# Who adds the two halves of a head pair's output: one addition of each pair moved from GpSimd to VectorE

## The chip, the cores and the metric

The kernel runs on one core of a Trainium2 chip. The time is the device time of one execution in microseconds (us). Each kernel is timed several times, and the median counts. Beside that, one execution is recorded by the hardware profiler. The engines are TensorE (PE; PEld is its loading of weights), VectorE (DVE), ScalarE (ACT), GpSimd (POOL) and SyncE (SP), which issues the DMAs.

## What is computed

Two layers, each an attention block and a gated MLP block with a mixing over the sequence, over 2048 tokens of width 640. The change touches attention only. It has 32 heads of 20 numbers, and the 2048 tokens are cut into 4 segments of 512. Within a segment attention is causal softmax; across segments a memory M is read.

```python
for s in range(N):                       # 4 segments
    qs, ks, vs = q[:, :, s], k[:, :, s], v[:, :, s]
    logits = jnp.einsum("bhqd,bhkd->bhqk", qs, ks) * scale + mask
    p = _softmax(logits, axis=-1)
    a_dot = jnp.einsum("bhqk,bhkd->bhqd", p, vs)
    pq = phi(qs)
    num = jnp.einsum("bhld,bhde->bhle", pq, M)
    den = jnp.einsum("bhld,bhd->bhl", pq, z)[..., None] + 1e-6
    a_mem = num / den
    o = g * a_mem + (1.0 - g) * a_dot
    outs.append(o)
    pk = phi(ks)
    M = M + jnp.einsum("bhld,bhle->bhde", pk, vs)
    z = z + jnp.einsum("bhld->bhd", pk)
```

## The kernel before

Each layer runs three stages one after the other: attention (phase1a), the MLP's input half (phase1b) and its spatial half with the output (phase2). Some work of phase1b is already placed into the end of attention.

Attention goes over 64 pairs of heads per layer: segment by segment, and in a segment through 16 pairs. Two pairs take five steps (the loop over t in `run`). For each pair TensorE makes the scores twice. Once by queries (`by_queries`), into the PSUM tile mp, of which there is one buffer; VectorE takes the row maxima of it (mxs, lines 956 and 959). These are turned on TensorE (mtp), split into two float16 parts (mr, ScalarE and VectorE) and written by DMA into spare rows of qk, so that the second making of the scores, by keys (`by_keys`, into es), has the maximum already subtracted. ScalarE takes the exponential of es into P (line 933). P is float32; it is split into two float16 parts, PH by ScalarE (line 968) and the rest PL = P - PH by GpSimd (line 970, two instructions of 128x640 for each head, so four for a pair; the last two pairs of a layer's second heads are done by VectorE). TensorE multiplies PH and PL with the values (`pvs`, line 998) into the PSUM tile pv, one buffer, 41 columns for each head and block of 128 queries: 20 columns of the values' high part, one column of sums of P, and 20 columns of the values' low part.

`combine` makes a pair's output from pv. VectorE scales the sums (rs, line 1009), inverts them (1010) and multiplies all of pv by them into ab in SBUF (1014). With a the first 20 columns of ab and b the last 20, the output is a + b, plus what was read from the memory if the segment isn't the first. The memory's part lies already in the group's tile gm (`read`, written by VectorE at line 834), of which o is the pair's slice. GpSimd does both additions: line 1017 adds o to a (only for segments after the first), line 1018 puts a + b into o. When the last pair of a group of 6 or 8 heads is done, `out` splits gm into two float16 parts, ohl (ScalarE at line 1026, GpSimd at line 1027), and SP stores them (line 1030).

Between these steps TensorE gets filler: the projections of queries and keys (kps, qps), of values (vps) and of the output (yps), the memory's update (mup) and reading (num). VectorE and ScalarE finish each of them (qhl, khl, relu, phq, phl, vs). Layernorm of coming rows is spread over VectorE, ScalarE and GpSimd as well (lnst, lnrs, xnhl).

TensorE's order in attention is that of the program. The order on the other engines comes from the scheduler, which works with its own model of time: where an instruction is moved or gone, others may change places. Each engine then works through its own order and waits at each instruction for what it needs.

Of the kernel before, what the change touches and what calls it, by code (L numbers as in the profile page):

```python
# [14 lines left out]
ALU = mybir.AluOpType  # L15
# [578 lines left out]
class Attention:  # L594
# [407 lines left out]
    def combine(self, n, s, m, h0):  # L1002
        g, nc = self.g, self.nc
        T = self.pv.pop(n)
        if (s, m) not in self.gm:
            self.gm[s, m] = self.pl3.tile([128, 4, 8, DH], F32, tag="gm", name="gm")
        ot = self.gm[s, m]
        rs = self.pl2.tile([128, 4, 2], F32, tag="rs", name="rs")
        nc.vector.tensor_tensor(rs, T[:, :, :, DH], g.iomg[:, h0:h0 + 2].unsqueeze(1).to_broadcast((128, 4, 2)), ALU.mult)
        nc.vector.reciprocal(rs, rs)  # L1010
        c = h0 - UH[m][0]
        o = ot[:, :, c:c + 2, :]
        ab = self.pl2.tile([128, 4, 2, 41], F32, tag="ab", name="ab")
        nc.vector.tensor_tensor(ab, T, rs.unsqueeze(3).to_broadcast((128, 4, 2, 41)), ALU.mult)  # L1014
        a, b = ab[:, :, :, 0:DH], ab[:, :, :, DH + 1:]
        if s > 0:
            nc.gpsimd.tensor_tensor(a, a, o, ALU.add)
        nc.gpsimd.tensor_tensor(o, a, b, ALU.add)
        if h0 + 2 < UH[m][-1] + 1:
            return  # L1020

        def out():
            nh = len(UH[m])
            hl = self.e2.tile([128, 2, D], F16, tag="xh", name="ohl")[:, :, :4 * nh * DH].rearrange("p i (t h d) -> p i t h d", t=4, d=DH)
            oh, ol = hl[:, 0], hl[:, 1]
            nc.scalar.copy(oh, ot[:, :, :nh, :])
            nc.gpsimd.tensor_tensor(ol, ot[:, :, :nh, :], oh, ALU.subtract)
            c = slice(UH[m][0] * DH, (UH[m][0] + nh) * DH)
            for i, o in enumerate((oh, ol)):
                nc.sync.dma_start(self.o_d[s][:, i, c].rearrange("(t p) c -> p t c", p=128), o.rearrange("p t h d -> p t (h d)"))  # L1030

        self.post(2, out)
# [229 lines left out]
```

## Time and profile before

| | us |
|---|---|
| three runs | 2304.68, 2308.20, 2310.23 |
| median | 2308.20 |
| the profiled execution | 2313.21 |
| its span, first to last instruction | 2311.5 |

An execution shows busy time for each engine, groups of instructions by line, a list of which engine waited for which, and the chain of work that ended last. A group's row gives line, engine, operation, output and inputs with shapes, how many there are, their busy time and the mean of one in ns, and how long the engine stood idle just before them with what ended that. In a timeline a row gives start, duration, and in brackets the idle time ahead of it. A time in attention of layer 0 lies between about 60 and 620 us, in layer 1 between about 1190 and 1735 us.

### The profile page before, as it was taken

Reading aid. Unit: us, or ns where it says so; the run is one execution under the profiler, and the core shown is the slowest. Engines: PE = TensorE matmul, PEld = TensorE weight load, DVE = VectorE, ACT = ScalarE, POOL = GpSimd, SP = SyncE. Lnnn points to the kernel's source line nnn. Section 1 sums busy time; section 2 is a strip of 40 time slices with the busy share of each in tenths; the row PEclk is TensorE's granted clock in tenths of the full one; section 3 lists DMA queues with packets and bytes.
Section 4 is the critical chain, followed back from the end, with each engine's and each line's share of the span. In section 5 each row is a group of like instructions: output and inputs, shape, how many; then the busy total and the mean of one; then the engine's idle time right before and its main releaser. Section 6 shows DMA issues by size and latency. Waiting matters only on the chain.

```text
span 2311.5 us, 52604 instructions
## 1 busy us (share of the span) xinstructions
PE 2167.8 (94%) x21706; PEld 1306.2 (57%) x21706; DVE 1372.8 (59%) x2577; ACT 1139.0 (49%) x1344; POOL 987.0 (43%) x976
## 2 busy tenths in 40 slices
PE   5888889999899999999998989999989999999998
PEld 3455555666555555555554556566665555555554
DVE  7678878777754544343327786777756443534331
ACT  3578788888532322121126987888863322212110
POOL 2387889999610000000104988899991100000000
PEclk9999999999899999999999999999999999999999
DMA  5566665345743687566634465443565347756561
GB/s 167 148 159 157 169 165 133 84 119 133 212 127 86 150 231 158 160 156 162 148 86 107 113 149 144 124 102 106 139 172 127 94 118 201 164 155 163 154 147 47
DMA packets 512113, 325.60 MB, mean 141 GB/s; under 512 B 411488, under 2 KB 454368, under 8 KB 507520
## 3 DMA queue, kind: packets, MB, share of 16 engines
q1 hardware_dynamic: 511872, 322.23, 54.5%
q8 instruction: 170, 2.79, 0.5%
q14 instruction: 71, 0.58, 0.1%
HBM read 148.46 MB, written 85.61 MB: 101 GB/s over the span
## 4 chain that ended last, share of the span: by engine, by line
PE 56%; DMA 4%; POOL 4%; DVE 3%; ACT 3%; issue 2%; SPq 1%; DVEq 0%; ACTq 0%; POOLq 0%
PE gp L450 23%; PE zp L363 13%; PE cyp L479 8%; POOL PL L970 3%; PE qps L756 2%; PE pv L998 2%; PE vps L697 2%; PE kps L756 1%; PE mp L895 1%; DMA th<-xnhl 1%; PE yps L729 1%; PE yp L340 1%; ACT P L933 1%; PE es L895 1%; DVE mxs L959 1%
## 5 line engine op out<-in xcount | busy, mean ns | idle before, releaser
L970 POOL TENSOR_TENSOR PL<-P,PH 128x640 f16<-128x640 f32 x380 | 535.5, 1434 | 53.3 <-PE pv L998 43.6
L450 PE MATMUL gp<-zh,wt 128*128 128x432 f16 x2048 | 462.3, 346 | 0.0
L450 PEld LDWEIGHTS <-wt 128*128 128x128 f16 x3072 | 300.5, 98 | 257.6
L959 DVE TENSOR_REDUCE mxs<-mp 128x2 f32<-128x1024 f32 (+2 forms) x384 | 320.0, 861 | 140.5 <-PE mp L886 139.0
L933 ACT ACTIVATE P<-es,sc 128x1024 f32<-128x1024 f32 (+1 forms) x256 | 271.5, 1060 | 99.1 <-PE es L886 84.9
L465 POOL MEMSET un<- 128x64 f16 x32 | 5.0, 155 | 665.9 <-DMA ut<-un 632.7
L363 PEld LDWEIGHTS <-th 128*128 128x128 f16 x1920 | 188.6, 99 | 173.5 <-DMA th<-xnhl 9.7
L450 PE MATMUL gp<-zl,wt 128*128 128x432 f16 x1024 | 270.6, 346 | 0.0
L453 ACT ACTIVATE u<-gp,bsp,un 128x864 f32<-128x864 f32 x32 | 34.2, 1070 | 431.1 <-PE gp L450 419.6
L968 ACT CAST PH<-P 128x1280 f16<-128x1280 f32 x192 | 239.7, 1248 | 1.6
L272 POOL TENSOR_TENSOR lnrs<-lnve,mhalf 128x1 f32<-128x1 f32 x96 | 60.2, 635 | 421.2 <-DVE lnve L271 374.5
L427 DVE TENSOR_REDUCE am<-wr 128x1 f32<-128x2048 f32 x32 | 73.1, 2286 | 210.2 <-DMA wr<-in_B_w_sp_dram 210.2
L970 POOL TENSOR_TENSOR PL<-Pb,PH 128x640 f16<-128x640 f32 x124 | 177.1, 1454 | 12.4 <-PE pv L998 8.0
L697 PE MATMUL vps<-wvh,xt 128*128 128x320 f16 x640 | 156.6, 313 | 25.5 <-DVE relu L788 19.6
L479 PE MATMUL cyp<-wuh,ut 128*128 128x320 f16 (+1 forms) x896 | 165.1, 301 | 5.8 <-DMA ut<-un 5.8
L895 PEld LDWEIGHTS <-qk 64*128 64x128 f16 (+1 forms) x2048 | 78.2, 94 | 160.4 <-issue 140.0
L479 PEld LDWEIGHTS <-ut 128*128 128x128 f16 (+1 forms) x1344 | 132.1, 98 | 61.6 <-DMA ut<-un 6.6
L998 PE MATMUL pv<-vs,PL 128*128 128x41 f16 x2560 | 157.0, 181 | 4.7 <-POOL PL L970 4.3
L998 PE MATMUL pv<-vs,PH 128*128 128x41 f16 x2560 | 159.5, 182 | 1.1 <-DVE ab L1014 0.8
L363 PE MATMUL zp<-wi1h,th 128*128 128x432 f16 x640 | 151.2, 352 | 7.8 <-DMA th<-xnhl 7.6
L895 PE MATMUL es<-qk 64*128 64x512 f16 (+3 forms) x1024 | 124.8, 300 | 27.7 <-ACT P L933 20.1
L363 PE MATMUL zp<-wi0h,th 128*128 128x432 f16 x640 | 148.3, 346 | 0.0
(189 smaller groups left out, 4294.5 us busy)
## 6 DMA issues: line engine op xcount, KB each, us to landing
wr<-in_B_w_sp_dram SPq DMA_DIRECT2D x32, 1024.0 KB
qk<-st SPq DMA_DIRECT2D x256, 120.0 KB
z<-z SPq DMA_DIRECT2D x32, 432.0 KB
cz<-z SPq DMA_DIRECT2D x32, 432.0 KB
xt<-in_A_x_dram SPq DMA_DIRECT2D x32, 320.0 KB
st<-qhl SPq DMA_DIRECT2D x40, 256.0 KB
st<-khl SPq DMA_DIRECT2D x40, 256.0 KB
x<-x SPq DMA_DIRECT2D x32, 320.0 KB
```

The costliest lines, as they stand in the source:

```text
L363: nc.tensor.matmul(zp[:, n, :FHH], a[:, k, :], b[:, k, c:c + FHH], start=(k == 0 and j == 0), stop=(k == KD - 1 and j == 2))
L427: nc.vector.tensor_reduce(am, wr, AX.X, ALU.max, apply_absolute_value=True)
L450: nc.tensor.matmul(gp[:, n, :FHH], wt[:, k // 8, a, k % 8, :], b[:, k, n * FHH:(n + 1) * FHH], start=(k == 0 and j == 0), stop=(k == NT - ...
L479: nc.tensor.matmul(yp[:, n, :320], a[:kn[k], k, :], b[:kn[k], k, n * 320:(n + 1) * 320], start=(k == 0 and j == 0), stop=(k == KO - 1 and ...
L697: nc.tensor.matmul(ps, a[:, k, c], b[:, k, n * 320:(n + 1) * 320], start=(i == 0), stop=(i == 14))
L756: nc.tensor.matmul(ps, a[:, k, c], b[:, k, :], start=(i == 0), stop=(i == 14))
L895: nc.tensor.matmul(out[:, h, o:o + w], a[r, ac], b[r, bc], start=o == 0, stop=False, skip_group_check=True)
L933: g.exp = nc.scalar.activation(P, E, AF.Exp, scale=g.esc)
L959: e = nc.vector.tensor_reduce(mx[:, :, n, j], mp[:, :, o:o + w], AX.X, ALU.max)
L968: nc.scalar.copy(PH, P[:, h])
L970: (nc.gpsimd if h == 0 or n < self.N - self.TAIL else nc.vector).tensor_tensor(PL[:, c], P[:, h, c], PH[:, c], ALU.subtract)
L998: nc.tensor.matmul(pv[:, i, h, :], x[:, c:c + 128], v[:, j, h0 + h, :], start=(j == 0 and x is PH), stop=(j == i and x is PL), skip_group_ ...
```

## The change

```diff
         nc.vector.tensor_tensor(ab, T, rs.unsqueeze(3).to_broadcast((128, 4, 2, 41)), ALU.mult)
         a, b = ab[:, :, :, 0:DH], ab[:, :, :, DH + 1:]
+        nc.vector.tensor_tensor(a if s > 0 else o, a, b, ALU.add)
         if s > 0:
-            nc.gpsimd.tensor_tensor(a, a, o, ALU.add)
-        nc.gpsimd.tensor_tensor(o, a, b, ALU.add)
+            nc.gpsimd.tensor_tensor(o, a, o, ALU.add)
```

VectorE adds a and b right behind the multiplication that makes them (line 1016 of the changed kernel). In the first segment the result goes straight to o, and GpSimd does nothing for the pair. In the other segments it goes back to a, and GpSimd adds o (line 1018). Over both layers GpSimd goes from 96 + 128 additions to 96, and VectorE gets 128.

On VectorE, around the pair whose multiplication ends at 460.76 us in the profile (layer 0, third segment; the numbers behind the names are the program's buffers), before:

```order
L786 SCALAR_TENSOR_TENSOR phq_8161<-qps_7969,relu_8145 128x512
L1009 TENSOR_TENSOR rs_8240<-pv_8187,iomg_116 128x8
L1010 RECIPROCAL rs_8240<-rs_8240 128x8
L1014 TENSOR_TENSOR ab_8243<-pv_8187,rs_8240 128x328
L956 TENSOR_REDUCE mxs1_289<-mp_8247 128x2x2
L774 SCALAR_TENSOR_TENSOR khl_8280<-kps_8097,khl_8280 128x512
```

and now:

```order
L786 SCALAR_TENSOR_TENSOR phq_8161<-qps_7969,relu_8145 128x512
L1009 TENSOR_TENSOR rs_8240<-pv_8187,iomg_116 128x8
L1010 RECIPROCAL rs_8240<-rs_8240 128x8
L1014 TENSOR_TENSOR ab_8243<-pv_8187,rs_8240 128x328
L1016 TENSOR_TENSOR ab_8243<-ab_8243 128x8x20
L956 TENSOR_REDUCE mxs1_289<-mp_8247 128x2x2
L774 SCALAR_TENSOR_TENSOR khl_8280<-kps_8097,khl_8280 128x512
```

The addition L1016 stands between the multiplication and the reduce that frees mp. In most places it stands right behind L1014; in a few the scheduler puts another instruction between them.

On GpSimd at the same pair (ab_8243) and the pair before it (ab_8107, the last of its group), before:

```order
L1017 TENSOR_TENSOR ab_8107<-ab_8107,gm_7017 128x8x20
L1018 TENSOR_TENSOR gm_7017<-ab_8107 128x4x40
L970 TENSOR_TENSOR PL_8151<-P_281,PH_8150 128x640 x2
L1027 TENSOR_TENSOR ohl_8275<-gm_7017,ohl_8275 128x480
L1017 TENSOR_TENSOR ab_8243<-ab_8243,gm_7361 128x8x20
L970 TENSOR_TENSOR PL_8229<-P_281,PH_8228 128x640 x2
L1018 TENSOR_TENSOR gm_7361<-ab_8243 128x4x40
```

and now:

```order
L1018 TENSOR_TENSOR gm_7017<-ab_8107,gm_7017 128x4x40
L1027 TENSOR_TENSOR ohl_8275<-gm_7017,ohl_8275 128x480
L970 TENSOR_TENSOR PL_8151<-P_281,PH_8150 128x640 x2
L1018 TENSOR_TENSOR gm_7361<-ab_8243,gm_7361 128x4x40
L970 TENSOR_TENSOR PL_8229<-P_281,PH_8228 128x640 x2
```

One addition is left for each pair. It stands where L1017 stood, so that the two PL that stood between the additions of the second pair are now behind it; and ohl moved ahead of two PL.

On TensorE the order in attention is unchanged. In phase1b of layer 0 (zp is the input product, yp the output product of a later tile) it was:

```order
L363 MATMUL zp_11827<-wi0h,th 128x432
L340 LDWEIGHTS o
L340 MATMUL yp<-woh,o 128x320
L363 LDWEIGHTS th
L363 MATMUL zp_11872<-wi1h,th 128x432
```

and is:

```order
L363 MATMUL zp_11775<-wi1h,th 128x432
L340 LDWEIGHTS o
L340 MATMUL yp<-woh,o 128x320
L340 LDWEIGHTS o
L340 MATMUL yp<-woh,o 128x320
L340 LDWEIGHTS o
L340 MATMUL yp<-wol,o 128x320
L363 LDWEIGHTS th
L363 MATMUL zp_11827<-wi0h,th 128x432
```

The first matmuls of this yp stand one block of zp earlier; the rest of yp is unchanged but for a few more of its matmuls that are spread the same way.

## The prediction

> **What bounds the kernel now.** I read the page's busy times first, then the engines' busy time by stretches of the two attention stages, then what TensorE waits for.
>
> ```profile
> span 2311.5 us, 52604 instructions
> PE 2167.8 (94%) x21706; PEld 1306.2 (57%) x21706; DVE 1372.8 (59%) x2577; ACT 1139.0 (49%) x1344; POOL 987.0 (43%) x976
> ```
>
> TensorE is busy for 94% of the whole. The change lies in attention only, and there the picture is another one. The columns below are the stretch, its length, and the busy time of PE, PEld, DVE, ACT and POOL.
>
> ```profile
> 110.00:250.00 140.00, 119.77 (x1773) 72.11 (x1772) 116.72 (x221) 113.51 (x142) 110.89 (x96) 0.95 0.65 165
> 250.00:400.00 150.00, 130.43 (x1970) 84.85 (x1968) 119.85 (x212) 122.43 (x156) 129.88 (x119) 0.98 0.57 150
> 400.00:520.00 120.00, 116.49 (x1862) 76.75 (x1861) 86.80 (x166) 99.15 (x116) 115.94 (x110) 1.00 0.39 103
> 1600.00:1735.00 135.00, 123.67 (x2004) 84.39 (x1997) 90.91 (x177) 104.32 (x115) 126.28 (x121) 0.99 0.56 148
> sum 1035.00, PE 943.49 PEld 608.57 DVE 782.03 ACT 832.47 POOL 901.53; mean PE 117.94 PEld 76.07 DVE 97.75 ACT 104.06 POOL 112.69
> ```
>
> The last row sums eight stretches, 1035 us of attention in both layers (these four and 520 to 640, 1230 to 1365, 1365 to 1480, 1480 to 1600). GpSimd is busy for 901.53 of them, 87%, VectorE for 782.03, 76%. So GpSimd is the fuller one of the two, and the change carries work from the fuller to the emptier. But between 400 and 520 TensorE itself leaves only 3.5 of 120 us idle. Nothing gained elsewhere can bring more than that there. What TensorE stands waiting for says more (waiter, released by, total, times, longest):
>
> ```profile
> PE es L895 <- ACT P L933: 20.1, 27, 2.7
> PE vps L697 <- DVE relu L788: 19.6, 9, 3.9
> PE mp L895 <- DVE mxs L959: 8.9, 19, 1.7
> PE mup L849 <- DVE mr L981: 8.4, 8, 2.0
> PE es L895 <- ACT Pb L933: 6.8, 5, 3.1
> PE pv L998 <- POOL PL L970: 4.3, 6, 1.0
> ACT P L933 <- POOL PL L970: 13.3, 12, 2.2
> ACT P L933 <- PE es L886: 84.9, 99, 2.7
> ```
>
> For GpSimd TensorE waits 4.3 us in all, for VectorE 36.9 us in the three rows alone. GpSimd is full but seldom late; VectorE is less full and often late. This is why I expect little from the relief and something from the burden.
>
> **What is removed.**
>
> ```profile
> L970 POOL TENSOR_TENSOR PL<-P,PH 128x640 f16<-128x640 f32 x380 | 535.5, 1434 | 53.3 <-PE pv L998 43.6 <-ACT PH L968 6.3 <-ACT qps L783 2.5
> L1018 POOL TENSOR_TENSOR gm<-ab 128x160 f32<-128x160 f32 x128 | 64.7, 505 | 10.6 <-DVE ab L1014 6.7
> L1017 POOL TENSOR_TENSOR ab<-ab,gm 128x160 f32<-128x160 f32 x96 | 51.4, 535 | 8.3 <-DVE ab L1014 8.2
> L855 DVE TENSOR_TENSOR mst<-mup,bmask 128x168 f32<-128x168 f32 x18 | 5.8, 321 | 0.0
> ```
>
> GpSimd loses all 96 of L1017 and the 32 of L1018 that belong to the first segment: 51.4 + 32 x 0.505 = 67.6 us busy, about 0.5 us for each of 128 pairs. What of it reaches the end: at most TensorE's 4.3 us directly, and through ScalarE's 13.3 us of waiting for P. TensorE waits 26.9 us for ScalarE's exponentials while these wait 98.2 us themselves, so I pass on 27% of the 13.3: 3.6 us. With some 2 us for the drain at each stage's end, where the layernorm's GpSimd step is queued behind PL, I take **-10 us**; the ends are 0 and -17.6 (4.3 + 13.3, all of it).
>
> **What is added: 128 additions of 128x160 on VectorE.** Bare, one costs 0.32 us by the L855 row (168 elements, 0.321): 41 us of VectorE. But L855 reads one input from PSUM, and so does the L1014 before it. The new addition reads both inputs from SBUF. The nearest such instruction is L794, beside L774 of the same 512 elements with one input in PSUM:
>
> ```profile
> L774 DVE SCALAR_TENSOR_TENSOR qhl<-qps,qhl 128x512 f16<-128x512 f32 x40 | 27.2, 679 | 5.2 <-ACT qhl L770 4.2 <-ACT relu L773 1.0
> L794 DVE SCALAR_TENSOR_TENSOR phl<-relu,sc,phl x30: 741/1172/1957, 59.9 to 1518.8; 128x512 f16<-128x512 f32 x30
> 380.88 1.96 DVE L794 SCALAR_TENSOR_TENSOR phl<-relu,sc,phl 128x512 f16<-128x512 f32 x1
> 380.89 3.21 POOL L970 TENSOR_TENSOR PL<-P,PH 128x640 f16<-128x640 f32 x2 [2.68 <-PE pv L998]
> ```
>
> L774 always takes 0.68. L794 takes 0.74 at least, 1.17 in the median, 1.96 at most. The long one began at 380.88, beside a GpSimd PL that ran from 380.89; one PL takes 1.43, and L794 ended about 0.5 after the first of the two. So it stood until GpSimd's instruction was over, with some 0.2 of its 0.75 already behind it. GpSimd lost too: its two PL took 3.21 where two take 2.76 elsewhere (rows below), 0.45 for an instruction of 0.75, so that 0.3 of it cost GpSimd nothing.
>
> The Trainium skill ("SBUF — State Buffer", section "Who interferes with whom") says that a VectorE instruction with two SBUF inputs and a GpSimd instruction that reads SBUF contend, and that whichever is second blocks until the first is done. It speaks against this change, which makes 128 such instructions; the L794 rows agree, though no run yet shows it for an addition. By that rule the sum is the one with the wait below, without it the one with 8 us.
>
> How long an addition stands: GpSimd is busy 87% of the time, mostly with PL of 1.43 us, so what is left of the one in progress is 0.87 x 0.72 = 0.62 us on average, and 0.12 more for the rest of the addition. That is 0.75 us for each pair instead of 0.32, or 96 us of VectorE instead of 41, and VectorE goes from 782 to 878 of 1035 us, 85%. GpSimd should lose next to nothing by an instruction of 0.32.
>
> What of the 0.75 reaches TensorE depends on what is queued behind the addition on VectorE: mostly the reduce of the next mp, of which there is one buffer. Two places show both cases.
>
> ```profile
> 458.95 2.76 POOL L970 TENSOR_TENSOR PL<-P,PH 128x640 f16<-128x640 f32 x2 [1.25 <-ACT qps L783]
> 460.26 0.50 DVE L1014 TENSOR_TENSOR ab<-pv,rs 128x328 f32<-128x328 f32 x1
> 460.86 1.23 DVE L956 TENSOR_REDUCE mxs<-mp 128x4 f32<-128x1024 f32 x1
> 462.14 0.39 PE L895 MATMUL mp<-qk 60*128 60x512 f16 x2
> 463.10 0.39 PE L895 MATMUL es<-qk 64*128 64x512 f16 x2 [0.51 <-ACT Pb L933]
> ```
>
> L1014 ends at 460.76, GpSimd's PL at 461.71. The addition would end at 461.83, the reduce would start there and not at 460.86, and the matmuls into mp, which followed its end by 0.05, come some 1.0 us later. The es behind them waited 0.51 for ScalarE anyway, so about 0.5 stays.
>
> ```profile
> 444.72 0.50 DVE L1014 TENSOR_TENSOR ab<-pv,rs 128x328 f32<-128x328 f32 x1
> 444.42 2.76 POOL L970 TENSOR_TENSOR PL<-P,PH 128x640 f16<-128x640 f32 x2
> 446.17 1.23 DVE L956 TENSOR_REDUCE mxs<-mp 128x4 f32<-128x1024 f32 x1 [0.95 <-PE mp L886]
> ```
>
> Here the addition would stand from 445.22 to about 445.9, and the reduce waits for TensorE until 446.17: no cost. I went through all 128 places in this way:
>
> ```profile
> L1014 DVE TENSOR_TENSOR ab<-pv,rs x128: 481/500/501, 111.2 to 1731.8; 128x328 f32<-128x328 f32 x128
> ```
>
> Behind the end of each I laid the rest of GpSimd's instruction, let VectorE's idle time take it up, and counted what was left at a reduce beyond the time to the next matmul into mp, and at each row for which TensorE already waited. That gives 29 us; with the bare 0.32 it gives 8. Of the 29 I take 60%, **+17 us**, because at places like the first TensorE's waits for ScalarE take up part. The ends are 8 and 29.
>
> **What is moved.** Where the last pair of a group is added, the cast L1026 stands up to four places earlier on ScalarE, and with it the stores on SP. GpSimd's one addition now stands where L1017 stood, often two PL earlier, so the cast should not wait longer.
>
> ```profile
> ACT ohl L1026 <- POOL gm L1018: 13.7, 8, 6.3
> 627.90 2.53 SPq L328 DMA_TRANSPOSE o<-o  x1
> 653.53 0.30 PE L340 MATMUL yp<-woh,o 128*128 128x320 f16 x1
> ```
>
> That wait is 13.7 us of ScalarE now, and could shrink or grow by some 5 that I can't place: 0. On TensorE the first matmuls of yp come one block of 60 earlier (11 us) in layer 0; their o was fetched at 627.90, 25 us before the first of them ran: 0. L1018 now waits for VectorE's addition, with PL behind it, but GpSimd stood waiting for ab only 8.2 us in all (row L1017): under 2 us, inside the ends.
>
> **Sum.** -10 + 17 + 0 = +7. The profiled execution took 2313.2 (span 2311.5 and 1.7 around it), so 2320 for it; it lies 5.0 above the median of the runs, 2308.2, and by the median the forecast is **2315 us**.
>
> **The rivals.** (1) *GpSimd sets the pace, and its relief wins.* For it speaks the chain of waits in the last stretch of layer 1:
>
> ```profile
> by line: POOL PL L970 19.3%; PE yps L729 11.6%; PE pv L998 7.9%; issue 6.6%; DMA th<-xnhl 4.9%; PE mp L895 4.7%; ACT P L933 4.6%; ACT PH L968 4.4%; PE qps L756 4.3%; PE es L895 3.8%; POOL gm L1018 2.8%; PE kps L756 2.7%; POOL ab L1017 2.7%;
> ```
>
> L1017 is 2.7% of 135 us there, 3.6 us; if the stretch before gives as much and layer 0 the same, some 14 us go, less the 8 of bare additions: -6, 2302. It decides if TensorE's rows only look full while it follows GpSimd, and if the additions stand no longer than 0.32. Against it: the 4.3 us that TensorE waits for GpSimd. The Trainium skill ("Perfetto Trace Analysis", section "Identifying the Most-Contended Engine") says that matmul busy time misjudges TensorE, and that the engine of highest occupancy is to be relieved first; weight loads are 608.57 of 1035 us here, so by that rule GpSimd with 87% is it, and the result is this rival's.
>
> (2) *VectorE's idle time takes it all.* The additions stand as long as forecast, but reduces wait for TensorE before most of them, and the 17 shrink to the relief's 10: 2308, no change.
>
> (3) *The wait is passed on whole.* All of the 29 and no relief: +29, 2337. That decides if TensorE has no other wait behind it.
>
> That the addition isn't where the change says is no rival: the order shows 128 rows of it on VectorE.
>
> **How the numbers follow.** A measurement here tells 0.2%, 4.6 us, from no change. The forecast (slower by 5 to 20) gets 0.46, rival 3 0.09, together slower 0.55. Rival 2 and small sums of both signs get 0.25, rival 1 0.20. The range goes from 2301, rival 1, to 2335, near rival 3.
>
> **What would show it.** The new VectorE addition with a minimum near 0.3 and a mean near 0.75 us, its long ones ending just after a PL ends: the wait is right. Its mean at 0.32: rival 1 or 2. TensorE's waits for mxs and mr up from 17.3 us in both rows: the path is right; unchanged, and the time too: rival 2. PL's mean stays near 1.43; if it grows past 1.5, GpSimd pays for the port and I've missed a cost. Wrong altogether I would be if GpSimd's lead moves whole stages forward, which the stretches would show as shorter with TensorE no less busy.

## The result, and the profile after

The changed kernel took 2325.18 us in the median of four runs (2324.46 to 2328.94), the kernel before 2308.22 beside it. The ratio is 1.0073, with a 95% interval of 1.0058 to 1.0088: slower by 17 us, where 7 were forecast. The way was right, the range holds it, and the size was taken too small. The profiled execution took 2325.00 us. That of the kernel before took 2313.21, 5.0 above its median, so the two profiles lie only 11.8 us apart.

The page's span and busy times of the changed kernel, and its busy time in the eight stretches of attention (columns as in the prediction: PE, PEld, DVE, ACT, POOL):

```profile
span 2322.9 us, 52604 instructions
PE 2169.5 (93%) x21706; PEld 1308.0 (56%) x21706; DVE 1463.9 (63%) x2705; ACT 1141.4 (49%) x1344; POOL 933.2 (40%) x848
```

```profile
400.00:520.00 120.00, 114.34 (x1867) 75.78 (x1866) 99.76 (x181) 98.50 (x116) 106.50 (x91) 1.00 0.38 102
sum 1035.00, PE 934.05 PEld 601.88 DVE 862.36 ACT 825.92 POOL 842.53; mean PE 116.76 PEld 75.23 DVE 107.79 ACT 103.24 POOL 105.32
```

GpSimd gave up 59 us of 901 there (now 842.53) and VectorE took on 80. TensorE, which does the same work in all, is busy for 9 us less in the same stretches: it stands longer. Between 400 and 520, where it left 3.5 us idle before, it now leaves 5.7.

The groups of the changed kernel by line and shape (count, busy us and mean ns of one, idle time before them and what ended it), and behind them the view of line 1016 alone (shortest, median and longest in ns):

```profile
L1016 DVE TENSOR_TENSOR ab<-ab 128x160 f32<-128x160 f32 x96 | 82.6, 861 | 2.5
L1016 DVE TENSOR_TENSOR gm<-ab 128x160 f32<-128x160 f32 x32 | 17.0, 532 | 0.8
L970 POOL TENSOR_TENSOR PL<-P,PH 128x640 f16<-128x640 f32 x380 | 538.8, 1445 | 101.2 <-PE pv L998 82.7 <-ACT PH L968 14.6 <-ACT phl L793 1.9
L1018 POOL TENSOR_TENSOR gm<-ab,gm 128x160 f32<-128x160 f32 x96 | 50.9, 530 | 25.5 <-DVE ab L1016 25.2 <-DMA st<-qhl 0.3
```

```profile
L1016 DVE TENSOR_TENSOR ab<-ab x96: 304/735/1604, 255.8 to 1744.3; 128x160 f32<-128x160 f32 x96
L1016 DVE TENSOR_TENSOR gm<-ab x32: 302/475/1221, 109.5 to 1376.9; 128x160 f32<-128x160 f32 x32
```

The same 160 elements take between 0.30 and 1.60 us. All 128 additions stand for 99.6 us, 0.78 each. The multiplication ahead of them, also a TENSOR_TENSOR but with one of its inputs (pv) in PSUM, is even at all 128 places of the same execution:

```profile
L1014 DVE TENSOR_TENSOR ab<-pv,rs x128: 481/500/501, 108.3 to 1743.8; 128x328 f32<-128x328 f32 x128
```

GpSimd's PL takes 1445 ns where it took 1434, and GpSimd stands idle before it for 101 us, twice the 53 of before, most of it (82.7) for TensorE's pv: the relieved engine waits for TensorE.

Who waits for whom in the changed kernel (total, times, longest), the rows that the prediction read for the kernel before:

```profile
PE mp L895 <- DVE mxs L959: 21.1, 24, 1.8
PE mup L849 <- DVE mr L981: 14.1, 9, 2.5
PE es L895 <- ACT P L933: 12.8, 17, 2.9
PE mp L895 <- DVE mxs L956: 9.2, 14, 1.6
PE pv L998 <- POOL PL L970: 2.8, 3, 1.8
PE es L895 <- ACT Pb L933: 1.3, 1, 1.3
ACT P L933 <- POOL PL L970: 2.3, 4, 0.8
```

TensorE's waits for VectorE's maxima and mr (first, second and fourth row) are 44.4 us together. Before, L959 and mr made 17.3. With L956, which the prediction did not show, it was 20.1; its row before:

```profile
PE mp L895 <- DVE mxs L956: 2.8, 5, 1.6
```

TensorE's waits for ScalarE's exponentials are 14.1 after 26.9.

One collision, at the place that the prediction worked out (the pair whose multiplication ended at 460.76; it now ends at 464.12). Timeline of the changed kernel, start and duration:

```profile
462.57 2.77 POOL L970 TENSOR_TENSOR PL<-P,PH 128x640 f16<-128x640 f32 x2
463.62 0.50 DVE L1014 TENSOR_TENSOR ab<-pv,rs 128x328 f32<-128x328 f32 x1
464.16 1.36 DVE L1016 TENSOR_TENSOR ab<-ab 128x160 f32<-128x160 f32 x1
465.44 1.21 DVE L956 TENSOR_REDUCE mxs<-mp 128x4 f32<-128x1024 f32 x1
466.71 0.39 PE L895 MATMUL mp<-qk 60*128 60x512 f16 x2 [1.26 <-DVE mxs L956]
466.99 0.39 PE L895 MATMUL es<-qk 64*128 64x512 f16 x2
```

GpSimd's second PL ends at 465.34, the addition at 465.52, the reduce behind it starts then, and TensorE stands 1.26 us for it. Counted from the start of L1014, the matmuls into mp come 3.09 us later here and 1.88 before (462.14 - 460.26): 1.21 lost. Those into es come after 3.37, and after 2.84 before: 0.53 lost, since there they waited 0.51 for ScalarE and here for nothing. The prediction said 1.0 and 0.5 for this place, for an addition of 1.07 us; it took 1.36, since 1.22 us of the PL were left at the end of L1014 and not 0.95. So what it said of a single place held. What it made of the sum came out too small.

### The profile page after: what moved, and what is told of

Same layout as the page of the kernel before. It is cut to its first block, busy times and chain, and to the rows that moved or that the text cites. A ratio compares the mean times of both kernels' runs of the same rounds, so it can differ in the third digit from the quotient of the medians.

```text
span 2322.9 us, 52604 instructions
## 1 busy us (share of the span) xinstructions
PE 2169.5 (93%) x21706; PEld 1308.0 (56%) x21706; DVE 1463.9 (63%) x2705; ACT 1141.4 (49%) x1344; POOL 933.2 (40%) x848
## 4 chain that ended last, share of the span: by engine, by line
PE 66%; DVE 14%; DMA 7%; ACT 5%; issue 4%; POOL 3%; SPq 1%; DVEq 0%; ACTq 0%; POOLq 0%
PE gp L450 23%; PE zp L363 13%; PE cyp L479 8%; DVE mxs L959 4%; PE vps L697 3%; PE pv L998 3%; PE qps L756 3%; PE mp L895 3%; PE kps L756 2%; POOL PL L970 2%; PE yps L729 2%; PE es L895 2%; PE num L821 1%; ACT PH L968 1%; DMA th<-xnhl 1%
## 5 line engine op out<-in xcount | busy, mean ns | idle before, releaser
L970 POOL TENSOR_TENSOR PL<-P,PH 128x640 f16<-128x640 f32 x380 | 538.8, 1445 | 101.2 <-PE pv L998 82.7
L450 PE MATMUL gp<-zh,wt 128*128 128x432 f16 x2048 | 462.3, 346 | 0.0
L450 PEld LDWEIGHTS <-wt 128*128 128x128 f16 x3072 | 300.5, 98 | 257.6
L959 DVE TENSOR_REDUCE mxs<-mp 128x2 f32<-128x1024 f32 (+2 forms) x384 | 319.7, 860 | 113.5 <-PE mp L886 112.3
L363 PEld LDWEIGHTS <-th 128*128 128x128 f16 x1920 | 187.4, 98 | 171.2 <-DMA th<-xnhl 10.6
L450 PE MATMUL gp<-zl,wt 128*128 128x432 f16 x1024 | 270.6, 346 | 0.0
L895 PE MATMUL mp<-qk 60*128 60x512 f16 (+3 forms) x1024 | 127.5, 306 | 34.1 <-DVE mxs L959 21.1
```

The costliest lines, as they stand in the source:

```text
L363: nc.tensor.matmul(zp[:, n, :FHH], a[:, k, :], b[:, k, c:c + FHH], start=(k == 0 and j == 0), stop=(k == KD - 1 and j == 2))
L450: nc.tensor.matmul(gp[:, n, :FHH], wt[:, k // 8, a, k % 8, :], b[:, k, n * FHH:(n + 1) * FHH], start=(k == 0 and j == 0), stop=(k == NT - ...
L895: nc.tensor.matmul(out[:, h, o:o + w], a[r, ac], b[r, bc], start=o == 0, stop=False, skip_group_check=True)
L959: e = nc.vector.tensor_reduce(mx[:, :, n, j], mp[:, :, o:o + w], AX.X, ALU.max)
L970: (nc.gpsimd if h == 0 or n < self.N - self.TAIL else nc.vector).tensor_tensor(PL[:, c], P[:, h, c], PH[:, c], ALU.subtract)
```

## The experiments

The theory: the additions wait on VectorE for GpSimd's instructions (below, "the port"), and that wait reaches the end. Rivals: it is the load of 128 more instructions on VectorE, whatever they read; or it is the scheduler's new order of the program; or it is TensorE's granted clock, which differs a little from run to run. The ratios are against the kernel before, timed on the same chip. Profiles are single executions; the table gives four lengths from their timelines: from the first to the last reciprocal L1010 of a layer's 64 pairs, and from there to the first matmul of gp (L450), the join of attention to the MLP. Two profiles of one kernel (the change and its repeat) differ by up to 4 us in a row. The profiled execution of e2_relief lies 7.1 us above its kernel's median, that of e6_one_input 5.4 below.

| us | layer 0 pairs | layer 0 join | layer 1 pairs | layer 1 join |
|---|---|---|---|---|
| before | 504.7 | 188.4 | 477.8 | 191.4 |
| the change | 512.4 | 185.6 | 486.3 | 190.9 |
| e5_after_again | 516.3 | 187.1 | 487.1 | 189.5 |
| e6_one_input | 504.5 | 187.4 | 475.8 | 188.7 |
| e2_relief | 505.0 | 187.7 | 471.7 | 190.8 |
| e3_burden2 | 513.7 | 201.0 | 488.5 | 201.2 |
| e4_burden1 | 502.5 | 198.8 | 477.0 | 201.7 |
| e9_late | 529.2 | 187.2 | 490.0 | 188.8 |
| e11_late_one | 501.0 | 186.9 | 474.5 | 189.9 |
| e1_reduce | 511.8 | 194.0 | 475.7 | 195.1 |
| e8_psum | 514.4 | 185.2 | 485.6 | 184.7 |
| e12_late_reduce | 510.0 | 194.2 | 480.0 | 194.5 |

**The port alone (e5_after_again, e6_one_input).** The first is the change itself once more. The second differs from it in one instruction:

```diff
-        nc.vector.tensor_tensor(a if s > 0 else o, a, b, ALU.add)
+        nc.vector.tensor_reduce(a if s > 0 else o, a.unsqueeze(4), AX.X, ALU.add)
```

> The changed kernel itself, on the chip of the next three, as their yardstick: +17 us, +-4, by every theory.

> The changed kernel with the addition replaced by a reduce over an axis of one element: the same 160 elements, the same place, every engine's order the same, but one SBUF input; b is left out of the output. Port theory: 0.32 us at every place instead of 0.78 on average, and 15 to 20 us less than the changed kernel, -3 to +3 us against the kernel before. Load theory: 10 to 15 us of the loss stay, only some 3 to 5 come back. Schedule theory: no change against the changed kernel, +17 us.

The change came to 2332.61 us, ratio 1.0096 (1.0083 to 1.0109), a little above the 17 +-4 expected; the one-input form, which leaves b out of the output, came to 2310.91, 1.0004 (0.9994 to 1.0013). The instructions stand in the same order on every engine of the two kernels. Line 1016 of e6_one_input, and then its waits:

```profile
L1016 DVE TENSOR_REDUCE ab<-ab x96: 297/320/321, 253.1 to 1727.8; 128x160 f32<-128x160 f32 x96
```

```profile
PE es L895 <- ACT P L933: 18.4, 22, 3.1
PE mp L895 <- DVE mxs L959: 11.2, 18, 1.7
PE mup L849 <- DVE mr L981: 9.9, 7, 2.1
PE mp L895 <- DVE mxs L956: 4.2, 7, 1.6
PE es L895 <- ACT Pb L933: 2.0, 2, 1.7
```

With one input in SBUF the instruction never takes more than 0.321 us, and the loss of attention is gone (504.5 and 475.8 in the table). So the port costs 1.0096 - 1.0004 = 0.92%, 21 us (some 17.5 to 25 with both intervals). What the change has beside it, the relief, the bare load and the new order, comes to no difference together. TensorE's waits for VectorE fall from 44.4 to 25.3, those for ScalarE come back from 14.1 to 20.4.

A part of the 21 us goes with the granted clock. It was 0.981 to 0.984 in the four runs of the change and 0.982 to 0.988 in the twelve of the one-input form. The profiled ones had 0.983 and 0.988. In them TensorE was busy for 2174.1 and 2164.4 us with the same work, 9.7 apart, and idle (span less busy) for 155.7 and 139.0, 16.7 apart. The runs of the two kernels at 0.982 to 0.984 took 2331.91 to 2335.43 (three) and 2310.05 to 2317.66 us (five), with 16 us between the medians. So the wait itself makes some 16 to 17 us, and the clock can't be the whole of it. Whether the longer standing also lowers the clock, no run shows.

**What VectorE's time is worth without the port (e7_tiny).** As e6_one_input, but of 8 elements in the later segments:

```diff
-        nc.vector.tensor_reduce(a if s > 0 else o, a.unsqueeze(4), AX.X, ALU.add)
+        n = 1 if s > 0 else DH
+        nc.vector.tensor_reduce((a if s > 0 else o)[:, :, :, 0:n], a[:, :, :, 0:n].unsqueeze(4), AX.X, ALU.add)
```

> As the one before, but for segments after the first the reduce takes 8 elements instead of 160, about 0.15 us instead of 0.32 (b and most of the sum are left out). The orders in attention are nearly those of the changed kernel. Port theory: 2 to 5 us below the kernel with 160 elements, since bare load costs little: -3 to -8 against the kernel before. Load theory: 8 to 12 us below it, half of the load gone. Schedule theory: +17 us.

2306.09 us, ratio 0.9979 (0.9969 to 0.9990). The 96 took 0.167 us each, 14.4 us of VectorE less in all, and the kernel became 5.8 us shorter by the ratios (0.25%; 2.5 to 9 with both intervals), between the two expectations: 0.4 us for each us of VectorE. That is a rough figure: unlike e6_one_input, this kernel's order differs from the change's at a few places on TensorE and VectorE, and the two profiled executions, both at a clock of 0.988, have spans of 2303.4 and 2304.0.

**The relief alone (e2_relief).** From the kernel before:

```diff
-        if s > 0:
-            nc.gpsimd.tensor_tensor(a, a, o, ALU.add)
-        nc.gpsimd.tensor_tensor(o, a, b, ALU.add)
+        nc.gpsimd.tensor_tensor(o, a, o if s > 0 else b, ALU.add)
```

> The kernel before without line 1017's work and with nothing added on VectorE: for segments after the first GpSimd does one addition (a + o) and the low half b is left out of the output. Port theory with the terms of the prediction: the relief alone gives -10 us (ends 0 and -17.6), and the burden is then 27. If TensorE's 4.3 us of waiting for GpSimd are all there is to win: -4 us. Schedule theory: slower than before, by up to 17, since GpSimd's, ScalarE's and SP's orders move here as they do in the change.

2302.34 us against 2311.62, ratio 0.9967 (0.9952 to 0.9982): 7.6 us shorter by the ratio, 9.3 by the medians. The kernel leaves b out of the output of the later segments. Its waits:

```profile
PE es L895 <- ACT P L933: 14.3, 20, 1.6
PE mup L849 <- DVE mr L981: 8.4, 8, 2.0
PE mp L895 <- DVE mxs L959: 8.0, 15, 1.7
PE es L895 <- ACT Pb L933: 4.4, 5, 2.7
PE mp L895 <- DVE mxs L956: 3.2, 6, 1.6
```

VectorE's rows stay at 19.6 (20.1 before). ScalarE's go from 26.9 to 18.7: this is where the relief goes, through P. So 8.2 of the 26.9 us in which a later burden could have hidden are used by the relief itself.

**The burden alone (e3_burden2, e4_burden1).** To the kernel before, which keeps all of GpSimd's additions, one VectorE instruction is added, with two inputs in SBUF or with one; the result goes to a tile that nobody reads:

```diff
+        nc.vector.tensor_tensor(self.dum, a, b, ALU.add)          # e3_burden2
+        nc.vector.tensor_reduce(self.dum, a, AX.X, ALU.add)       # e4_burden1
```

> The kernel before with GpSimd's additions kept, and on VectorE an extra addition of a and b (two SBUF inputs, 160 elements) into a scratch tile that nobody reads. Port theory: mean of the extra addition 0.75 to 0.85 us, time +22 to +30 us. Load theory: +8 to +20, and about the same as with a single input. Schedule theory: under +5 us, as the orders hardly move.

> The kernel before with GpSimd's additions kept, and on VectorE an extra reduce of a (one SBUF input, 160 elements, same place) into a scratch tile that nobody reads. Port theory: 0.30 to 0.35 us at every place and time +4 to +9 us, a third of the extra addition's. Load theory: the same loss as with the extra addition, within 4 us. Schedule theory: under +5 us for both.

2354.21 us, ratio 1.0185 (1.0167 to 1.0204), and 2331.17, 1.0092 (1.0074 to 1.0109), both far above what was expected (22 to 30 us, and 4 to 9). The group of each:

```profile
L1017 DVE TENSOR_TENSOR dum<-ab 128x160 f32<-128x160 f32 x128 | 107.8, 843 | 3.2
```

```profile
L1017 DVE TENSOR_REDUCE dum<-ab 128x8 f32<-128x160 f32 x128 | 40.5, 316 | 3.2
```

The orders of these two are identical, so their difference is the port alone again: 23 us, by the table 11.2 and 11.5 in the two attentions. (The granted clock was 0.978 to 0.982 in the one and 0.981 to 0.984 in the other.) But e4 itself is no measure of the load. It loses nothing among the pairs (502.5 and 477.0) and 10 us at each join: the scheduler, given another instruction, put the blocks of phase1b in another order on TensorE, whose waits for their input (zp behind the DMA of th) rise from 7.6 us in the kernel before to 24.2. Here, unlike in the change, the rival of the order holds. TensorE's waits for VectorE and ScalarE in e3_burden2 (its lines stand one further down):

```profile
PE mp L896 <- DVE mxs L960: 24.2, 28, 3.0
PE mup L850 <- DVE mr L982: 16.5, 10, 2.8
PE es L896 <- ACT P L934: 13.9, 17, 2.3
PE mp L896 <- DVE mxs L957: 7.5, 13, 1.6
PE es L896 <- ACT Pb L934: 2.1, 1, 2.1
```

**In the first segment only (e10_first).** The kernel before, with VectorE's addition where GpSimd has no second one:

```diff
-        nc.gpsimd.tensor_tensor(o, a, b, ALU.add)
+            nc.gpsimd.tensor_tensor(o, a, b, ALU.add)
+        else:
+            nc.vector.tensor_tensor(o, a, b, ALU.add)
```

> The change for the first segment only (32 of 128 pairs; VectorE does a + b, GpSimd nothing); the other segments as before. In the changed kernel's profiles the 16 pairs of the first segment lose 2 to 3 us per layer. Port theory: +3 to +6 us, since GpSimd is emptier there and the additions stand only 0.52 us. If the relief of GpSimd pays in the first segment: -4 to 0.

2313.14 us against 2312.38, ratio 1.0008 (0.9995 to 1.0022): the 32 additions took 0.537 us in the mean, and no difference can be told, where the port theory had 3 to 6 us. The loss of the change is mainly in the later segments, where the additions stand 0.86.

**Another place (e9_late, e11_late_one).** The change with the addition one step later in the program; the second with the one-input form in it:

```diff
-        nc.vector.tensor_tensor(a if s > 0 else o, a, b, ALU.add)
-        if s > 0:
-            nc.gpsimd.tensor_tensor(o, a, o, ALU.add)
+        def add():
+            nc.vector.tensor_tensor(a if s > 0 else o, a, b, ALU.add)
+            if s > 0:
+                nc.gpsimd.tensor_tensor(o, a, o, ALU.add)
+        self.post(1, add)
```

> The changed kernel with the same additions handed out one step later, so that the reduce of the next mp stands ahead of the addition on VectorE and not behind it. If the port's wait costs time because that reduce is queued right behind it (the path that the prediction named): the additions still stand 0.7 to 0.85 us on average, but a good half of the 20 us goes: +3 to +10 us against the kernel before. If any VectorE time lost to the port costs the same wherever it stands: +15 to +22.

> The late kernel with one SBUF input in the addition's place (160 elements, every engine's order the same, b left out). Port theory: 0.32 us at every place. If the place behind the reduce makes the wait cheap, the two late kernels differ by 5 to 10 us; if the port's wait costs the same wherever it stands, by about 20, as in the first place.

2348.78 us against 2312.38, ratio 1.0162 (1.0138 to 1.0187): twice the loss, which neither expectation had. With one input, and b left out of the output, 2306.30, ratio 0.9976 (0.9962 to 0.9990), in the same orders on all engines. So the later place is a good one, but for the port, which costs 42 us there. In the two profiled executions, at granted clocks of 0.983 and 0.989, 32.1 of it is TensorE's idle time (173.6 and 141.5) and 11.2 its busy time. The view of the addition's line in e9_late, and behind it one case of its timeline:

```profile
L1018 DVE TENSOR_TENSOR ab<-ab x96: 303/1133/1562, 274.3 to 1769.3; 128x160 f32<-128x160 f32 x96
L1018 DVE TENSOR_TENSOR gm<-ab x32: 313/1394/1525, 115.3 to 1409.4; 128x160 f32<-128x160 f32 x32
```

```profile
553.09 1.29 DVE L959 TENSOR_REDUCE mxs<-mp 128x2 f32<-128x768 f32 x2 [0.42 <-PE mp L886]
554.11 2.85 POOL L970 TENSOR_TENSOR PL<-P,PH 128x640 f16<-128x640 f32 x2 [2.88 <-PE pv L998]
554.29 1.40 DVE L1018 TENSOR_TENSOR ab<-ab 128x160 f32<-128x160 f32 x1
```

The addition begins 0.18 us after a PL has begun and stands until it is over. That is frequent there: 106 of the 128 stand right behind a reduce L959, and 60 take over 1.3 us, most of them begun 0.12 to 0.22 us after a GpSimd instruction (in the change 26 of 128 take that long). In 43 of the 60 the PL had waited for matmuls of pv, and the addition stands behind the reduce of mp, which TensorE fills. That TensorE so starts both side by side is the likely reason why they meet so often; no run tests it. In all the additions of e9_late stand 128.7 us against 39.4 in e11, 89 us more for 42 us of time; in the change it is 99.6 against 40.4 in e6, 59 us more for 21.

**Versions without the port that compute the whole output (e1_reduce, e8_psum, e12_late_reduce).** e1_reduce replaces the addition by one reduce over both halves of ab, 320 elements, one input:

```diff
-        nc.vector.tensor_tensor(a if s > 0 else o, a, b, ALU.add)
+        both = abw.rearrange("p t h (i d) -> p t h d i", i=2)[:, :, :, 0:DH, :]
...
+        nc.vector.tensor_reduce(a, both, AX.X, ALU.add)
```

> The changed kernel, but VectorE sums the two halves by a reduce over pairs (one input, from SBUF, 320 elements) instead of an addition with two SBUF inputs. Port theory (the addition stands until GpSimd's instruction is over, and that is most of the loss): the reduce takes 0.45 to 0.5 us at every place, with no long ones; VectorE's work for it falls from 99.6 to about 62 us, and of the 17 us lost against the kernel before some 10 come back: 0 to +8 us (ratio 1.000 to 1.0035). Load theory (VectorE has more to do ahead of the reduce of mp, and the waits fall into idle time): a floor of 0.48 instead of 0.30 makes it no better than the changed kernel: +15 to +22 us. Schedule theory (other instructions that changed places cost the time): +17 us, as the places stay.

2328.63 us, ratio 1.0081 (1.0064 to 1.0099), as slow as the change. A miss, and by another way: the instruction takes 0.494 us, evenly, and the second layer's pairs lose nothing (475.7); but the order changed here too, TensorE's wait for th is 13.5 us (7.6 before), the joins lose 5.6 and 3.7, and the first layer's pairs 7.1. How much of these 7.1 comes from the order and how much from an instruction of 0.49 us, no run separates. e8 adds in PSUM, before the normalisation, and then multiplies half as many elements:

```diff
+        nc.vector.tensor_reduce(su, T.rearrange("p t h (i d) -> p t h d i", i=2)[:, :, :, 0:DH, :], AX.X, ALU.add)
...
+        nc.vector.tensor_tensor(a, su, rs.unsqueeze(3).to_broadcast((128, 4, 2, DH)), ALU.mult)
```

> A version that never reads two large inputs from SBUF: VectorE first sums the two halves in PSUM by a reduce (320 elements, one PSUM input, into free columns of the same bank), then multiplies 160 elements by rs; GpSimd does one addition as in the change. VectorE takes about 0.48 + 0.32 us for a pair instead of 0.50 + 0.78 in the changed kernel and 0.50 in the kernel before. Port theory: as with 0.3 us of bare load, -3 to +5 us against the kernel before. Load theory: +10 to +17. pv stays held 0.3 us longer, which all theories take as under 2 us.

2323.36 us, ratio 1.0045 (1.0029 to 1.0061), 10 us and not the -3 to 5 of the port theory. Its group by line, and two of its waits:

```profile
L1006 DVE TENSOR_REDUCE pv<-pv 128x160 f32<-128x320 f32 x128 | 62.6, 489 | 22.3 <-PE pv L997 21.2
```

```profile
PE pv L997 <- DVE ab L1016: 7.9, 6, 2.4
PE pv L997 <- DVE gm L1016: 7.3, 6, 2.9
```

No port, but VectorE now holds pv, of which there is one buffer, for the reduce and the multiplication, and TensorE waits 15.2 us for it where it waited 0.8 (L1014, before): attention loses 17.5 us, and the joins give 10 back. e12 puts the one-input addition into the later place of e11:

```diff
+        abw = self.pl2.tile([128, 4, 2, 62], F32, tag="ab", name="ab")
+        ab, a = abw[:, :, :, 0:41], abw[:, :, :, 42:62]
...
+            nc.vector.tensor_reduce(a if s > 0 else o, both, AX.X, ALU.add)
...
+        self.post(1, add)
```

> A kernel that computes the whole output: the addition stands one step later, as in e9_late, and is done by one instruction with one SBUF input, a reduce over both halves (320 elements, 0.49 us by e1_reduce's row), which writes 20 further columns of the same tile. If GpSimd's port was what e9_late lost, the addition keeps about 0.49 us at every place (no tail above 0.6) and nothing waits for GpSimd. Against e11_late_one (0.9976 of the kernel before, 0.31 us for one) VectorE has 0.18 x 128 = 23 us more; by what 14.4 us of VectorE were worth between e6_one_input and e7_tiny (5.8 us) that is some 9 us: 1.001, so about equal to the kernel before and clearly under the change (1.007 to 1.010). If the late place has room for it: 0.998. The rival is the order behind attention: two blocks of matmuls of the hidden layer (L363) change places on TensorE against e9_late; if that costs what it did in e1_reduce and e4_burden1, the joins are 5 to 10 us longer each and the ratio is 1.005 to 1.010.

2331.55 us against 2308.97, ratio 1.0088 (1.0073 to 1.0103), as the rival had it. The addition is even:

```profile
L1019 DVE TENSOR_REDUCE ab<-ab x96: 477/495/505, 263.1 to 1749.4; 128x160 f32<-128x320 f32 x96
```

Against e11 its pairs lose 9.0 and 5.5 us for 24 us more of VectorE, 0.6 for each where I had reckoned with 0.4, and its joins 7.3 and 4.6. No version of these beats the kernel before.

## Why the prediction was right, and where it was too small

- **The bound.** Right. TensorE waited little for GpSimd and much for VectorE, and that told the sign against the two shares of busy time (87% and 76%). By the rule of the Trainium skill ("Perfetto Trace Analysis", section "Identifying the Most-Contended Engine"), the engine of highest occupancy is relieved first; here that relief alone brought 7.6 us (e2_relief), and the work put on the emptier engine cost more.
- **The relief, -10.** Measured -7.6 (-11.1 to -4.2), and by the path given: ScalarE's wait for PL falls from 13.3 us to 2.4 in e2_relief (2.3 in the change). The 2 us taken for the drains do not show clearly: the joins of e2_relief are 0.7 and 0.6 shorter.
- **The duration, 0.75 us.** Measured 0.778, shortest 0.302. The 92 additions above 0.35 us all end 0.18 us after a GpSimd instruction has ended. PL went from 1.434 to 1.445, so GpSimd pays almost nothing. The Trainium skill ("SBUF — State Buffer", section "Who interferes with whom") has a VectorE instruction with two SBUF inputs contend with a GpSimd instruction that reads SBUF, and a reduce never; both now stand in runs, the addition here and the reduce in e6_one_input.
- **The bare addition, 8.** It fits: e6_one_input (1.0004) and e2_relief (0.9967) differ by 0.37%, 8.5 us (4 to 13 with both intervals), though they ran on two chips.
- **The share that is passed on, 60% of 29: the term that was mis-sized.** 17 was taken; the runs give 24.5 by the first timing (1.0073 - 0.9967 = 1.06%) and 29.8 by the second (1.0096), so five sixths of the walk's 29 or all of it. By the timings 21 of it is the port (e5 and e6) and 8 the load. TensorE's idle time (span less busy) grew by less: 136.3 us in the profile of e2_relief, 153.4 in the change and 155.7 in its repeat, that is 17.1 and 19.4 in these single executions, close to the 17. The sum had no term for the granted clock, with which a part of the rest goes ("The port alone"). So the waits were nearly right, and the step from them to the whole time was too small.
- **The reason given for the 60%**, that "TensorE's waits for ScalarE take up part", is right for a part. At the place shown they do: 1.21 us late became 0.53. But that place was taken from a trace without the relief. Against e2_relief, where GpSimd is already relieved, VectorE's three rows rise by 24.8 us (19.6 to 44.4), and ScalarE's two fall by 4.6 (18.7 to 14.1), a fifth and not two fifths. Without the relief, in e3_burden2, the three rows rise by 28.1 (20.1 to 48.2) and ScalarE's two fall by 10.9 (26.9 to 16.0), two fifths. So in these rows the prediction counted the slack once for the relief and once more for the burden. That this makes the difference in time is not shown: all of TensorE's idle time rose by only 17.1 against these 24.8, so other waits gave way as well.
- **What is moved, 0.** Right in the sum: the joins are no longer than before (185.6 and 190.9). ScalarE's wait of 13.7 us for gm became 19.9 (12.0 for L1018 and 7.9 for L1016), and GpSimd waits 25.2 us for the addition, where it had waited 8.2 for ab and the prediction took under 2 us of loss. No cost of it is seen at TensorE: its wait for PL is 2.8 (5.5 in the repeat) after 4.3.
- **The rivals.** The first (GpSimd sets the pace, 2302) had the sign of the relief, but took it for 14 where it was 7.6, and the additions do not stand at 0.32. The second (VectorE's idle time takes it) falls with the waits for mxs and mr, up by 17.9 us in the two rows named. The third (passed on whole) was right in its main part and wrong in giving no relief; -8 + 29 would have been 2329.
- **The chances.** "Slower by 5 to 20" had 0.46. The first timing lies in it with 17 us, the repeat, with 22, just outside, and both lie in the range. The two errors, a relief taken too large and a burden taken too small, go the same way, so nothing evened out by luck.

What stays open: why the same two kernels differ by 1.0073 in one timing and by 1.0096 in another. Their intervals just meet, and the granted clock of the change was 0.983 to 0.989 in the first and 0.981 to 0.984 in the second, which can be a part of it.

## What to carry to other kernels

Before an element-wise step goes from GpSimd to VectorE, see where its inputs lie: with two in SBUF it stood here until GpSimd's running instruction was over, and the price is what is left of that instruction, as far as something queued behind it is waited for. Look for a form with one SBUF input, and in the trace for a place where GpSimd has not just begun something long. Such a form may still cost more than it saves, as the three whole versions here did. And where a change both relieves and burdens, the slack that hides the one should not be counted again for the other.

## What the hardware showed beside it

When an addition and a GpSimd instruction start within some 25 ns of each other, the recorded starts do not tell which one is blocked. In the changed kernel an addition and a PL start nearly together at two places (the PL rows join two instructions each):

```profile
536.00 2.87 POOL L970 TENSOR_TENSOR PL<-P,PH 128x640 f16<-128x640 f32 x2
537.30 0.32 DVE L1016 TENSOR_TENSOR ab<-ab 128x160 f32<-128x160 f32 x1
```

```profile
571.00 2.76 POOL L970 TENSOR_TENSOR PL<-P,PH 128x640 f16<-128x640 f32 x2
572.34 1.60 DVE L1016 TENSOR_TENSOR ab<-ab 128x160 f32<-128x160 f32 x1
```

At the first, the second PL begins 60 ns behind the addition: the addition takes its 0.32, and the two PL 2.87 where they take 2.76 elsewhere, so GpSimd pays 0.11 us. At the second it begins 15 ns behind the addition by the records, and still VectorE stands for 1.60 us, longer than the PL itself. Of the 14 additions in this trace behind which a GpSimd instruction began 9 to 110 ns later, two were blocked so, at 15 and 16 ns; one at 9 ns and all from 25 ns on were not. The repeat has it otherwise: there the additions at 14, 15 and 17 ns were not blocked, and of two at 25 ns one was, for 1.60 us.
